# Attention of later blocks two chunks a stop, inside a y, with outputs in the h bank that is free

## The chip, the cores and the metric

The kernel runs on one core of one Trainium2 chip. A core has five engines with a queue each, worked through in order: TensorE (PE: matrix products, with weight loads in a row of their own, PEld), VectorE (DVE), ScalarE (ACT), GpSimd (POOL) and SyncE (SP, which only issues transfers here). Engines wait for each other by semaphores. Matmuls write PSUM; the kernel holds eight tiles of 128 x 512 floats there, called banks here. The metric is the time of one execution in microseconds (us), the median of several runs.

## The reference, cut to what matters

```python
# attention: B, H, S, D = 2, 8, 768, 64, blocks of 64 positions
intra = einsum('bhic,bhjc->bhij', qb, kb) * Dmask      # scores times powers of lam
intra = einsum('bhij,bhjd->bhid', intra, vb)
inter = einsum('bhid,bhde->bhie', qb * lam_pow, kv_state)
out   = intra + inter
kv_state = lam_block * kv_state + einsum('bhsd,bhse->bhde', kb * rev_pow, vb)
# then two feed-forward layers over 1536 tokens, 512 -> 2048 -> 512
h = x @ w_in;  g = elu(h);              x = g @ w_out
h = x @ w_in;  g = P(h) / (Q(h) + 1e-6);  y = g @ w_out  # P cubic, Q of |h| and h*h
```

## The kernel before, in words

The 1536 tokens lie in three blocks of T = 512 (t = 0, 1, 2), and the 2048 hidden features in 16 steps f of 128. A layer is a loop over t and f. A step issues on TensorE h(f) (`mlp_h`, 12 matmuls of 128 x 512, L435: three parts of a product that is split into high and low halves, four slices of the model width each) and then y(f - 2) (`mlp_y`, again 12, L517, into four banks that collect y over all f). Between them ScalarE and VectorE make g from h: L448 and L449 on ScalarE, L450 on VectorE, L452 on ScalarE (high half), L453 on VectorE (low half). Two banks with the tag "h" take turns; four belong to y; the last two, pa0 and pa1, are left for the attention.

Weights of layer 0 come packed and are unpacked on the way in block t = 0: L78, L81 and L84 on VectorE build the weight w_f of a step, L127 on ScalarE makes its high half and L128 on VectorE its low half; h(f + 2) is the first that needs them. In block t = 1 the weights of layer 1 are unpacked by the same three lines and parked in memory (`park_w2`).

The attention of block 0 is done in the start-up, in chunks of 128 positions. That of blocks 1 and 2 is woven into layer 0: chunks 8 to 23 of 64 positions (CS = 64, KB = 12 chunks in a batch) are worked on in t = 0 and 1, one at each of 17 stops (`att_visit`), f = 3, 5, 7, 9, 10, 12, 13, 14, 15 in t = 0 and f = 2, 4, 6, 8, 10, 12, 14, 15 in t = 1. A stop stands between h(f) and y(f - 2). `sm_products(n, d)` issues its matmuls of 64 x 64: for the new chunk n the scores (L340, into half 0 of aa0), and for the chunk d of the stop before the scores times values (L345, half 0 of aa1), the keys' product that goes into the state (L351, half 1 of aa0) and the state times queries (L356, half 0 of aa1). They are issued in pairs that lie in different quarters of the array, 8 steps for a chunk's L340 with L345 and 8 for its L351 with L356. Behind it VectorE masks the scores (L376), POOL scales the queries by the powers in qpow (L371), ScalarE brings out the output (L384, to xr) and VectorE adds up the state (L388); ScalarE scales keys (L365) and state (L395). At the first stop alone, two picks (L333) bring the powers for the other half of the rows into half 1 of aa1, and ScalarE copies them to qpow (L335).

The order within an engine is that of the code in a section under `manual_schedule`; operations of the lists `old`, `new`, `now` and `lows` are placed by hand around the stop. At the start of a block's layer 0, `x_split` makes the halves of x (L57 on ScalarE, L58 on VectorE). SP issues its transfers in the order of the code, and waits with each until its buffer is free.

Of the kernel before, what the change touches and what calls it, by code (L numbers as in the profile page):

```python
# [8 lines left out]
F32 = mybir.dt.float32  # L9
# [20 lines left out]
def fused_kernel(ctx, tc, lam, qkv, w1, w2, ab, out):  # L30
# [16 lines left out]
    ph = ctx.enter_context(tc.tile_pool(name="ph", bufs=2, space=PSUM))  # L47
# [252 lines left out]
    aa_tiles = []  # L300

    def sm_load_qk(k):
# [10 lines left out]
        for b in range(2):  # L313
            chunk[k + b] = {"q": qk[:, :, 0, b * CS:(b + 1) * CS],
                            "k": qk[:, :, 1, (1 - b) * CS:(2 - b) * CS]}

    def sm_load_kv(k):
        c, b, row = k // 2, k % 2, 4 * P
        chunk[k]["kv"] = kv = qq.tile([P, NP, 2, D], F32, tag="kv", name=f"kv{k}")
# [7 lines left out]
    def sm_products(n, d):  # L327

        if not aa_tiles:
# [5 lines left out]
            nc.scalar.activation(out=qpow[:, :, 0:CS], in_=aa_tiles[1][:, 1], func=AF.Copy)  # L335
        pn, pd = chunk.get(n), chunk.get(d)
        for m in range(NP):
            if pn:
                for r in ROWS:
                    nc.tensor.matmul(aa_tiles[0][r, 0, m], lhsT=pn["k"][r, m],  # L340
                                     rhs=pn["q"][r, m], start=True, stop=True,
                                     skip_group_check=True)
            if pd:
                for i, r in enumerate(ROWS):
                    nc.tensor.matmul(aa_tiles[1][ROWS[1 - i], 0, m], lhsT=pd["kv"][r, m, 1],  # L345
                                     rhs=pd["s"][r, m], start=m == 0, stop=d % KB == 0,
                                     skip_group_check=True)
        for m in range(NP):
            if pd and d % KB < KB - 1:
                for r in ROWS:  # L350
                    nc.tensor.matmul(aa_tiles[0][r, 1, m], lhsT=pd["kv"][r, m, 0],  # L351
                                     rhs=pd["kv"][r, m, 1], start=True, stop=True,
                                     skip_group_check=True)
            if pd and d % KB:
                for i, r in enumerate(ROWS):
                    nc.tensor.matmul(aa_tiles[1][ROWS[1 - i], 0, m], lhsT=state[r, m, 0],  # L356
                                     rhs=pd["q"][r, m], start=False, stop=True,
                                     skip_group_check=True)

    def sm_decay_k(n):  # L360

        kv = chunk[n]["kv"]
        if n % KB < KB - 1:
            for m in range(NP):
                nc.scalar.activation(out=kv[:, m, 0], in_=kv[:, m, 0], func=AF.Copy,  # L365
                                     scale=mask64[:, m, CS - 1:CS])

    def sm_decay_q(n):
        q = chunk[n]["q"]
        if n % KB:  # L370
            nc.gpsimd.tensor_tensor(out=q, in0=q, in1=qpow[:, :, 0:CS], op=ALU.mult)  # L371

    def sm_mask(n):
        b = chunk[n]
        b["s"] = s = ap_.tile([P, NP, CS], F32, tag="s", name=f"s{n}")
        nc.vector.tensor_tensor(out=s, in0=aa_tiles[0][:, 0], in1=mask64[:, :, 0:CS], op=ALU.mult)  # L376

    def sm_out(d):

        t, js = d * CS // T, slice(d * CS % T, d * CS % T + CS)  # L380
        if t not in xraw:
            xraw[t] = xr.tile([P, NP, T], F32, tag="xr", name=f"xr{t}")
        first, last = d % KB == 0, d % KB == KB - 1
        nc.scalar.activation(out=xraw[t][:, :, js], in_=aa_tiles[1][:, 0], func=AF.Copy)  # L384
        if first:
            nc.scalar.activation(out=state[:, :, 0], in_=aa_tiles[0][:, 1], func=AF.Copy)
        elif not last:
            nc.vector.tensor_tensor(out=state[:, :, 0], in0=aa_tiles[0][:, 1],  # L388
                                    in1=state[:, :, 1], op=ALU.add)

    def sm_decay_state(d):

        if d % KB not in (0, KB - 1):
            for m in range(NP):
                nc.scalar.activation(out=state[:, m, 1], in_=state[:, m, 0], func=AF.Copy,  # L395
                                     scale=qpow[:, m, CS - 1:CS])

# [102 lines left out]
    def mlp_y(layer, t, f):  # L500
# [27 lines left out]
    with ExitStack() as actx:  # L528
# [4 lines left out]
        qq = actx.enter_context(tc.tile_pool(name="qq", bufs=2))  # L533

# [20 lines left out]
        dmask = ac.tile([P, H, C + 1], F32, name="dmask")  # L555
        qpow = ac.tile([P, NP, C], F32, name="qpow")
        state = ac.tile([P, NP, 2, D], F32, name="state")

        mask64 = dmask.rearrange("p (m h) i -> p m h i", h=2)[:, :, 1, CS:]
# [8 lines left out]
        def make_qpow():  # L568
# [5 lines left out]
            def double(n):  # L574
# [4 lines left out]
        yy, hh = ((py, "y"),) * 2, ((ph, "h"),) * 2  # L579
        pp = (yy, hh, yy, yy, hh, yy, yy, ((ph, "h"), (pa, "pa0")))  # L580
# [4 lines left out]
        loads = [[(sm_load_qk, first), (sm_load_kv, first)], [(sm_load_kv, first + 1)],  # L585
                 [(sm_load_qk, first + 2)]]
        loads += [[(sm_load_kv, k + 1)] + [(sm_load_qk, k + 2)] * (k % 2 == 0 and k + 2 < end)
                  for k in range(first + 1, end - 1)]
        with tc.manual_schedule():
# [17 lines left out]
            for load, k in loads.pop(0):  # L607
                load(k)
# [294 lines left out]
```

## Time and profile before

| | |
|---|---|
| median of 3 runs | 571.9 us (571.89 to 572.04) |
| profiled execution, its own time | 572.56 us |
| span of its profile | 570.8 us |
| TensorE busy | 564.6 us (99%) |
| VectorE busy | 464.7 us (81%) |
| ScalarE busy | 358.5 us (63%) |
| GpSimd busy | 29.8 us (5%) |

A row of a timeline gives the start in us, the duration, the engine, the line and what it writes from what, and in brackets the idle time before it with what ended it. Neighbouring instructions of one kind are merged into one row (x4). A matmul of 64 x 64 in floats of 32 bits stands as two instructions in the trace. In the chain of work that ended last a piece's duration is the time from its start to the start of the next piece, so its rows add up without overlap.

### The profile page before, as it was taken

The numbers are of one execution on the slowest core, as the hardware profiler recorded it, in microseconds if no ns is written. First come the engines' busy times: TensorE is split into PE (matmuls) and PEld (weight loads), VectorE is DVE, ScalarE is ACT, GpSimd is POOL, SyncE is SP. The second block draws the span as 40 slices with busy tenths as digits, with TensorE's granted clock in tenths as the row PEclk, the third lists the DMA queues.
The fourth block names the chain that finished last, engine by engine and source line by source line (L and its number), as shares of the span: only waits on it lengthen the run. The fifth ranks groups of instructions, "written<-read, shape, count | busy, mean of one in ns | idle before, by whom it ended". The sixth has DMA issues, their size and how long they took to land.

```text
span 570.8 us, 9255 instructions
## 1 busy us (share of the span) xinstructions
PE 564.6 (99%) x3550; PEld 464.9 (81%) x3550; DVE 464.7 (81%) x722; ACT 358.5 (63%) x690; POOL 29.8 (5%) x51
## 2 busy tenths in 40 slices
PE   8999999999999999999999999999999999999997
PEld 7877888888888888888888888888888888888885
DVE  6999999965676635877979999888898888898882
ACT  3746646875554545555568976667877666776672
POOL 7401001100100000000000000000000000000000
PEclk9999999999999999999999999999999999999999
DMA  8977677464687513434432500000400000200001
GB/s 291 318 225 243 237 227 214 107 206 128 204 240 229 165 49 136 167 135 177 150 108 78 182 3 1 1 2 0 145 3 2 0 1 0 75 0 1 1 1 74
DMA packets 41215, 64.58 MB, mean 113 GB/s; under 512 B 20178, under 2 KB 20178, under 8 KB 41170
## 3 DMA queue, kind: packets, MB, share of 16 engines
q1 hardware_dynamic: 41168, 63.98, 35.8%
q8 instruction: 28, 0.46, 0.3%
q14 instruction: 17, 0.14, 0.1%
q10 hardware_dynamic: 2, 0.00, 0.0%
HBM read 53.48 MB, written 10.49 MB: 112 GB/s over the span
## 4 chain that ended last, share of the span: by engine, by line
PE 98%; DMA 1%; SPq 0%; ACT 0%; issue 0%
PE h L435 46%; PE y L517 43%; PE y L426 3%; PE aa L340 1%; DMA att<-qkv_in 1%; PE aa L351 1%; PE pa L243 1%; PE pa L209 1%; PE pa L249 0%; PE aa L356 0%; PE aa L345 0%; SPq L192 0%; PE sums L256 0%; PE pa L291 0%; ACT o L487 0%; PE aa L333 0%
## 5 line engine op out<-in xcount | busy, mean ns | idle before, releaser
L435 PE MATMUL h<-xhi,w 128*128 128x512 f32 x768 | 204.8, 389 | 0.0
L517 PE MATMUL y<-ghi,w 128*128 128x512 f32 x712 | 191.8, 392 | 0.0
L435 PEld LDWEIGHTS h<-xhi,w 128*128 128x128 f32 x768 | 143.8, 188 | 30.3 <-DVE w L128 0.4
L517 PEld LDWEIGHTS y<-ghi,w 128*128 128x128 f32 x712 | 132.3, 188 | 27.8
L435 PE MATMUL h<-xlo,w 128*128 128x512 f32 x384 | 102.6, 389 | 0.0
L517 PE MATMUL y<-glo,w 128*128 128x512 f32 x356 | 95.3, 389 | 0.0
L435 PEld LDWEIGHTS h<-xlo,w 128*128 128x128 f32 x384 | 72.1, 188 | 15.0
L517 PEld LDWEIGHTS y<-glo,w 128*128 128x128 f32 x356 | 66.8, 188 | 14.2
L461 ACT ACTIVATE a<-h,babs 128x512 f32<-128x512 f32 x48 | 33.0, 688 | 63.8 <-PE h L435 63.8
L448 ACT ACTIVATE a<-h 128x512 f32<-128x512 f32 x48 | 28.3, 589 | 43.1 <-PE h L435 42.9
L465 DVE SCALAR_TENSOR_TENSOR b<-b,babs,a 128x512 f32<-128x512 f32 x48 | 36.0, 751 | 20.9 <-ACT b L462 20.7
L450 DVE SCALAR_TENSOR_TENSOR b<-a,h 128x512 f32<-128x512 f32 x48 | 32.7, 681 | 15.3 <-ACT a L449 12.1
L452 ACT ACTIVATE ghi<-b 128x512 fp32r<-128x512 f32 x48 | 30.0, 626 | 22.4 <-DVE b L450 22.4
L453 DVE TENSOR_TENSOR glo<-b,ghi 128x512 fp32r<-128x512 f32 x48 | 34.0, 709 | 7.0 <-ACT ghi L452 4.8
L463 ACT ACTIVATE p<-h,cab 128x512 f32<-128x512 f32 x48 | 37.7, 785 | 0.0
L467 ACT ACTIVATE a<-b,one 128x512 f32<-128x512 f32 x48 | 35.0, 729 | 3.1 <-DVE b L465 2.6
L469 DVE SCALAR_TENSOR_TENSOR p<-p,cab,h 128x512 f32<-128x512 f32 x48 | 35.8, 746 | 1.2
L473 DVE SCALAR_TENSOR_TENSOR b<-b,one,a 128x512 f32<-128x512 f32 x48 | 35.8, 746 | 0.1
L475 DVE SCALAR_TENSOR_TENSOR p<-p,cab,a 128x512 f32<-128x512 f32 x48 | 35.8, 746 | 0.0
L58 DVE TENSOR_TENSOR glo<-p,ghi 128x512 fp32r<-128x512 f32 x48 | 33.0, 688 | 3.0 <-PE y L426 1.5
L468 DVE TENSOR_TENSOR p<-p,h 128x512 f32<-128x512 f32 x48 | 32.8, 682 | 2.9 <-ACT p L463 2.9
L477 DVE SCALAR_TENSOR_TENSOR p<-b,p 128x512 f32<-128x512 f32 x48 | 33.1, 690 | 1.2
(88 smaller groups left out, 611.2 us busy)
## 6 DMA issues: line engine op xcount, KB each, us to landing
raw<-w_in SPq DMA_DIRECT2D x64, 512.0 KB, 4.5
att<-qkv_in SPq DMA_DIRECT2D x16, 256.0 KB, 6.0
qk<-qkv_in SPq DMA_DIRECT2D x16, 256.0 KB, 4.3
kv<-qkv_in SPq DMA_DIRECT2D x64, 64.0 KB, 4.0
w2d<-wbuf SPq DMA_DIRECT2D x16, 256.0 KB, 4.5
wbuf<-w2d SPq DMA_DIRECT2D x16, 256.0 KB, 2.8
x2d<-o SPq DMA_DIRECT2D x12, 256.0 KB, 2.3
x2r<-x2d SPq DMA_DIRECT2D x12, 256.0 KB, 3.1
```

What stands on the lines that cost most here:

```text
L58: lo_eng.tensor_tensor(out=lo, in0=src, in1=hi.bitcast(F32), op=ALU.subtract)
L435: nc.tensor.matmul(h, lhsT=w[:, a, 0, k * P:(k + 1) * P], rhs=xs[layer, t, k][b], start=i == k == 0, stop=i == 2 and k == NP - 1)
L453: lambda: nc.vector.tensor_tensor(out=glo, in0=b, in1=ghi.bitcast(F32), op=ALU.subtract)]
L461: nc.scalar.activation(out=a, in_=h, func=AF.Abs, scale=babs[:, 0:1])
L463: nc.scalar.activation(out=p, in_=h, func=AF.Identity, scale=cab[:, 3:4], bias=cab[:, 2:3])
L465: nc.vector.scalar_tensor_tensor(out=b, in0=b, scalar=babs[:, 1:2], in1=a, op0=ALU.mult, op1=ALU.add)
L467: nc.scalar.activation(out=a, in_=b, func=AF.Ln, bias=one[:, 0:1])
L469: nc.vector.scalar_tensor_tensor(out=p, in0=p, scalar=cab[:, 1:2], in1=h, op0=ALU.add, op1=ALU.mult)
L473: nc.vector.scalar_tensor_tensor(out=b, in0=b, scalar=one[:, 0:1], in1=a, op0=ALU.add, op1=ALU.mult)
L475: nc.vector.scalar_tensor_tensor(out=p, in0=p, scalar=cab[:, 0:1], in1=a, op0=ALU.add, op1=ALU.mult)
L477: nc.vector.scalar_tensor_tensor(out=p, in0=b, scalar=2.0, in1=p, op0=ALU.subtract, op1=ALU.mult, reverse0=True)
L517: nc.tensor.matmul(ys[layer, t][m], lhsT=w[:, a, 1, m * P:(m + 1) * P], rhs=g[b], start=f == i == 0, stop=False)
```

## The change

Nine stops take the place of 17, at the steps s = 16 t + f of a list. Each stands inside a y, behind the second of its three parts (8 of 12 matmuls), and works on two chunks. The scores of both chunks n, n + 1 fill aa0 (L344). The keys' products (L359) are made for the chunks n - 1 and n, one chunk behind the loads rather than with the outputs, and lie in the two halves of aa1. The outputs of the two chunks of the stop before (L349, L364) go into a third place, `ax`: the h bank that the next h will take. One L395 of 128 x 512 brings them out, one mask L386 of 128 x 512 takes the place of two, and one L378 on POOL scales two chunks of queries. The state has a third copy, is summed in L405 (first time in L403) and scaled in L412; keys are scaled in L373. The large tables move into a weight slot; what the stops need of them lies in two small tiles (mask64, pow64), which two POOL copies and the one L335 fill. The banks for h have tags of their own, h0 and h1. In the new kernel L435 is L451, L517 is L533, and L448, L449, L450, L452, L453 are L464, L465, L466, L468, L469. TensorE's instructions of the stops, in the program's own count, go from 17 groups to nine.

```diff
-    ph = ctx.enter_context(tc.tile_pool(name="ph", bufs=2, space=PSUM))
+    ph = ctx.enter_context(tc.tile_pool(name="ph", bufs=1, space=PSUM))
...
-            nc.scalar.activation(out=qpow[:, :, 0:CS], in_=aa_tiles[1][:, 1], func=AF.Copy)
...
+            nc.scalar.activation(out=pow64, in_=aa_tiles[1][:, 1], func=AF.Copy)
+        if d is not None:
+            aa_x[0] = spare.rearrange("p (m x i) -> p m x i", x=2, m=NP)
+        for j in range(2):
+            pn = chunk.get(n + j) if n is not None else None
+            pd = chunk.get(d + j) if d is not None else None
+            for m in range(NP):
+                if pn:
+                    for r in ROWS:
+                        nc.tensor.matmul(aa_tiles[0][r, j, m], lhsT=pn["k"][r, m],
+                                         rhs=pn["q"][r, m], start=True, stop=True,
+                                         skip_group_check=True)
+                if pd:
+                    for i, r in enumerate(ROWS):
+                        nc.tensor.matmul(aa_x[0][ROWS[1 - i], m, j], lhsT=pd["kv"][r, m, 1],
+                                         rhs=pd["s"][r, m], start=j == m == 0,
+                                         stop=(d + j) % KB == 0, skip_group_check=True)
+        for j in range(2):
+            c = n + j - 1 if n is not None else None
+            kv = chunk[c]["kv"] if c in chunk and c % KB < KB - 1 else None
+            pd = chunk.get(d + j) if d is not None and (d + j) % KB else None
+            for m in range(NP):
+                if kv is not None:
+                    for r in ROWS:
+                        nc.tensor.matmul(aa_tiles[1][r, j, m], lhsT=kv[r, m, 0],
+                                         rhs=kv[r, m, 1], start=True, stop=True,
+                                         skip_group_check=True)
+                if pd:
+                    for i, r in enumerate(ROWS):
+                        nc.tensor.matmul(aa_x[0][ROWS[1 - i], m, j], lhsT=state[r, m, j],
+                                         rhs=pd["q"][r, m], start=False, stop=True,
+                                         skip_group_check=True)
...
+        nc.scalar.activation(out=xraw[t][:, :, js].rearrange("p m (b i) -> p m b i", b=2),
+                             in_=aa_x[0], func=AF.Copy)
...
+        tables = slot(1, [P, H * (C + 1) + NP * C], F32, "tables")
...
+        at = [3, 6, 9, 12, 14, NF + 2, NF + 6, NF + 10, NF + 14]
...
-        h_pool = lambda: (ph, "h")
+        h_pool = lambda: (ph, f"h{nh.pop()}")
+        nh = [f % 2 for f in range(2 * NF)][::-1]
...
+        def att_visit(s, f):
+
+            v = at.index(s)
+            spare = ph.tile([P, T], F32, tag=f"h{(f + 1) % 2}", name=f"ax{s}") if v else None
+            n = pairs[v] if v < len(pairs) else None
+            d = pairs[v - 1] if v else None
+            sm_products(n, d, spare)
+            if d is not None:
+                sm_out(d)
             if n is not None:
                 sm_mask(n)
                 sm_decay_q(n)
...
             if d is not None:
+                if n is not None:
+                    sm_state(n)
...
                 if len(queue) > LAG:
-                    mlp_y(*queue.pop(0))
+                    mlp_y(*queue.pop(0), between=(lambda: att_visit(s, f)) if s in at else None)
+                for load, k in loads.get(s, ()):
+                    load(k)
...
-    def mlp_y(layer, t, f):
+    def mlp_y(layer, t, f, between=None):
...
+            if between and i == 1:
+                between()
...
-        return ((ph, "h"), (ph, "h"), (pa, "pa0"), (pa, "pa1"))[nh[0] % 4]
+        return ((ph, "h0"), (ph, "h1"), (pa, "pa0"), (pa, "pa1"))[nh[0] % 4]
```

How the rows stand, at three places. In a name such as h_0_3 the numbers are block and step, and a number behind it the program's count of buffers.

TensorE at the first stop (f = 3), before: the end of h(3), the picks, the scores, and the start of y(1).

```order
L435 MATMUL h_0_3_586<-xhi_0_0_261,w_1_508 128x512 x2
L435 MATMUL h_0_3_586<-xhi_0_1_285,w_1_508 128x512 x2
L333 MATMUL aa_613<-dmask,tabs 64x256 x2
L340 MATMUL aa_612<-qk_200 64x64 x8
L517 MATMUL y_0_0_570<-ghi_0_1_504,w_1_508 128x512
L517 MATMUL y_0_1_571<-ghi_0_1_504,w_1_508 128x512
```

After, from the second part of y(1), with the semaphores that a row waits for in brackets (DMAHW: a transfer's):

```order
L533 MATMUL y_0_0_576<-glo_0_1_510,w_1_513 128x512 [waits DVE_50]
L533 MATMUL y_0_1_577<-glo_0_1_510,w_1_513 128x512
L533 MATMUL y_0_2_578<-glo_0_1_510,w_1_513 128x512
L533 MATMUL y_0_3_579<-glo_0_1_510,w_1_513 128x512
L333 MATMUL aa_640<-mask_162,tabs 64x256 [waits Pool_50] x2
L344 MATMUL aa_639<-qk_204 64x64 [waits DMAHW0_50,PE_50]
L344 MATMUL aa_639<-qk_204 64x64 [waits DMAHW1_50]
L344 MATMUL aa_639<-qk_204 64x64 x14
L359 MATMUL aa_640<-kv_207 64x64 [waits DMAHW2_50,Activation_50]
L359 MATMUL aa_640<-kv_207 64x64 [waits DMAHW4_50]
L359 MATMUL aa_640<-kv_207 64x64 x2
L359 MATMUL aa_640<-kv_207 64x64 [waits DMAHW3_50]
```

The scores and picks now stand inside y(1), and behind them L359, with a wait for ScalarE, stands ahead of y(1)'s last part.

ScalarE at the same stop, before: L448 and L449 belong to h(3), L335 is the copy of the picked powers.

```order
L448 ACTIVATE a_0_3_601<-h_0_3_586 128x512
L449 ACTIVATE a_0_3_601<-a_0_3_601 128x512
L335 ACTIVATE qpow<-aa_613 128x4x64
L365 ACTIVATE kv_203<-kv_203,dmask 128x64 x4
L127 ACTIVATE w_3_605<-w_3_606 128x1024
L452 ACTIVATE ghi_0_3_599<-b_0_3_602 128x512
```

After:

```order
L464 ACTIVATE a_0_3_610<-h_0_3_595 128x512
L465 ACTIVATE a_0_3_610<-a_0_3_610 128x512
L127 ACTIVATE w_3_614<-w_3_615 128x1024
L335 ACTIVATE pow_163<-aa_640 128x256
L468 ACTIVATE ghi_0_3_608<-b_0_3_611 128x512
```

The copy L335 moved from ahead of L127 of w_3 to behind it.

VectorE at the change from block 1 to block 2, before: L450 belongs to h(14) and h(15) of block 1, L58 makes the low half of x, L78, L81 and L84 unpack weights of layer 1.

```order
L450 SCALAR_TENSOR_TENSOR b_1_14_2479<-a_1_14_2478,h_1_14_2463 128x512
L453 TENSOR_TENSOR glo_1_14_2477<-b_1_14_2479,ghi_1_14_2476 128x512
L58 TENSOR_TENSOR xlo_2_0_2598<-xr_1715,xhi_2_0_2597 128x512 x2
L58 TENSOR_TENSOR xlo_2_1_2604<-xr_1715,xhi_2_1_2603 128x512 x2
L450 SCALAR_TENSOR_TENSOR b_1_15_2550<-a_1_15_2549,h_1_15_2534 128x512
L78 TENSOR_SCALAR wbuf<-raw_0_0_2627 128x512
L81 SCALAR_TENSOR_TENSOR wbuf<-raw_0_0_2627,wbuf 128x512
L453 TENSOR_TENSOR glo_1_15_2548<-b_1_15_2550,ghi_1_15_2547 128x512
L84 SCALAR_TENSOR_TENSOR wbuf<-raw_0_0_2627,wbuf 128x512
```

After (L466 is what L450 was, L469 what L453 was):

```order
L469 TENSOR_TENSOR glo_1_14_2479<-b_1_14_2481,ghi_1_14_2478 128x512
L78 TENSOR_SCALAR wbuf<-raw_0_0_2610 128x512
L81 SCALAR_TENSOR_TENSOR wbuf<-raw_0_0_2610,wbuf 128x512
L84 SCALAR_TENSOR_TENSOR wbuf<-raw_0_0_2610,wbuf 128x512
L78 TENSOR_SCALAR wbuf<-raw_0_1_2612 128x512
L58 TENSOR_TENSOR xlo_2_0_2580<-xr_1785,xhi_2_0_2579 128x512 x2
L58 TENSOR_TENSOR xlo_2_1_2586<-xr_1785,xhi_2_1_2585 128x512 x2
L466 SCALAR_TENSOR_TENSOR b_1_15_2549<-a_1_15_2548,h_1_15_2533 128x512
L81 SCALAR_TENSOR_TENSOR wbuf<-raw_0_1_2612,wbuf 128x512
```

Four steps on the weights moved ahead of L58 and of L466 of h(15).

## Rows read from the trace of the kernel before

**Rows 1.** The page: TensorE's busy time, and the shares of the chain by engine.
```profile
PE 564.6 (99%) x3550; PEld 464.9 (81%) x3550; DVE 464.7 (81%) x722; ACT 358.5 (63%) x690; POOL 29.8 (5%) x51
...
PE 98%; DMA 1%; SPq 0%; ACT 0%; issue 0%
```

**Rows 2.** Windows (columns: busy us of each engine): blocks 0 and 1.
```profile
36.00:72.00 36.00, 36.00 (x289) 29.25 (x286) 34.53 (x42) 22.73 (x51) 3.15 (x3) 1.00 0.74 237
...
118.00:224.00 106.00, 106.00 (x903) 86.60 (x902) 65.01 (x111) 54.12 (x128) 6.22 (x7) 1.00 0.55 162
```

**Rows 3.** The chain in order of time (start us, us, what): block 0, some pieces.
```profile
35.58 0.58 PE aa L333 x4
...
45.01 2.95 PE h L435 x12
...
52.03 2.72 PE h L435 x12
...
60.19 0.20 PE aa L340 x2
...
60.41 0.04 PE aa L340 x2
...
61.28 2.95 PE y L517 x12
```

**Rows 4.** Timeline of ScalarE (start us, us, instruction [idle before]): h(3), first stop.
```profile
38.90 0.63 ACT L449 ACTIVATE a<-a 128x512 f32<-128x512 f32 x1
39.44 0.37 ACT L335 ACTIVATE qpow<-aa 128x256 f32<-128x256 f32 x1
...
43.05 1.06 ACT L127 ACTIVATE w<-w 128x1024 fp32r<-128x1024 f32 x1 [2.29 <-DVE w L84]
```

**Rows 5.** Timeline of VectorE: the same stretch.
```profile
39.12 0.69 DVE L453 TENSOR_TENSOR glo<-b,ghi 128x512 fp32r<-128x512 f32 x1
39.72 0.42 DVE L376 TENSOR_TENSOR s<-aa,dmask 128x256 f32<-128x256 f32 x1
40.05 1.70 DVE L81 SCALAR_TENSOR_TENSOR w<-raw,w 128x1024 int32<-128x1024 int32 x1
41.79 1.22 DVE L84 SCALAR_TENSOR_TENSOR w<-raw,w 128x1024 int32<-128x1024 int32 x1
...
44.88 0.70 DVE L78 TENSOR_SCALAR w<-raw 128x1024 int32<-128x1024 int32 x1 [1.26 <-DMA raw<-w_in]
45.49 1.22 DVE L128 TENSOR_TENSOR w<-w,w 128x1024 fp32r<-128x1024 f32 x1
```

**Rows 6.** Timelines: VectorE's L84 of f = 6; ScalarE's eviction of a bank.
```profile
59.85 1.23 DVE L84 SCALAR_TENSOR_TENSOR w<-raw,w 128x1024 int32<-128x1024 int32 x1
...
224.56 0.61 ACT L487 ACTIVATE o<-y 128x512 f32<-128x512 f32 x1
```

**Rows 7.** Timelines at the end of block 1: VectorE, SP's loads.
```profile
211.48 2.50 DVE L58 TENSOR_TENSOR xlo<-xr,xhi 128x512 fp32r<-128x512 f32 x4 [5.16 <-ACT xhi L57]
...
215.16 0.43 DVE L78 TENSOR_SCALAR wbuf<-raw 128x512 int32<-128x512 int32 x1 [0.58 <-PE y L517]
215.62 0.69 DVE L81 SCALAR_TENSOR_TENSOR wbuf<-raw,wbuf 128x512 int32<-128x512 int32 x1
...
210.45 1.69 SPq L114 DMA_DIRECT2D raw<-w_in  x2
```

**Rows 8.** Windows of the program's end (PEclk: granted clock); timeline of TensorE's start.
```profile
566.00:567.00 1.00, 0.85 (x4) 0.38 (x2) 0.00 (x0) 0.24 (x2) 0.00 (x0) 1.00 0.35 131
...
569.00:570.00 1.00, 0.00 (x0) 0.00 (x0) 0.00 (x0) 0.00 (x0) 0.00 (x0) 1.00 0.07 23
570.00:570.50 0.50, 0.00 (x0) 0.00 (x0) 0.00 (x0) 0.00 (x0) 0.00 (x0) 0.59 0.00 0
...
5.92 1.13 PE L243 MATMUL pa<-att 128*64 128x128 f32 x8
...
9.17 0.66 PE L243 MATMUL pa<-att 128*64 128x128 f32 x8
```

More of the change, by code (lines that the diff above doesn't have):

```diff
@@ L348, in sm_products @@
[L348 to L358, printed above, removed]
+            nc.scalar.activation(out=pow64, in_=aa_tiles[1][:, 1], func=AF.Copy)
@@ L391, in sm_decay_state, with sm_state @@
-    def sm_decay_state(d):
-        if d % KB not in (0, KB - 1):
+        nc.scalar.activation(out=xraw[t][:, :, js].rearrange("p m (b i) -> p m b i", b=2),
+                             in_=aa_x[0], func=AF.Copy)
+    def sm_state(n):
+        if n - 1 in chunk and n % KB:
+            j = n % 2
+            if n % KB == 1:
+                nc.scalar.activation(out=state[:, :, j], in_=aa_tiles[1][:, j], func=AF.Copy)
+            else:
+                nc.vector.tensor_tensor(out=state[:, :, j], in0=aa_tiles[1][:, j],
+                                        in1=state[:, :, 2], op=ALU.add)
@@ L584, in fused_kernel @@
         first, end = todo[0], todo[-1] + 1
[L585 to L588, printed above, removed]
+        at = [3, 6, 9, 12, 14, NF + 2, NF + 6, NF + 10, NF + 14]
+        pairs = list(range(first, end, 2))
+        loads = {}
+        for i, k in enumerate(pairs[1:]):
+            s0 = at[i] if i else 1
+            for j, load in enumerate(((sm_load_kv, k - 1), (sm_load_qk, k), (sm_load_kv, k))):
+                loads.setdefault(s0 + (j if i == 0 else j // 2), []).append(load)
+        loads.setdefault(at[-2], []).append((sm_load_kv, end - 1))
+        work, late, states = {}, {}, {}
+        for v, s in enumerate(at[:-1]):
+            k = first + 2 * v
+            if v:
+                late.setdefault(s - 1, []).append((sm_decay_k, k - 1))
+                work.setdefault(s, []).append((sm_decay_k, k))
+            work.setdefault(s + 1, []).append((sm_decay_state, k))
+            states[s + 1] = k + 1
+            work.setdefault(s + 2 + (s + 2 == NF), []).append((sm_decay_state, k + 1))
         with tc.manual_schedule():
@@ L606, in fused_kernel @@
             load_pair(1)
-            for load, k in loads.pop(0):
-                load(k)
+            for load in (sm_load_qk, sm_load_kv):
+                load(first)
             def s_part(i):
@@ L711, in fused_kernel @@
         queue = []
-        def att_visit(due, more):
-            n = todo.pop(0) if more and todo else None
-            d = due.pop() if due else None
-            sm_products(n, d)
+        def att_visit(s, f):
[6 more added lines that the diff above has]
+                sm_out(d)
             if n is not None:
@@ L792, in fused_kernel @@
                                 FULL + 1: (FULL + 3, NF - 3)}[f])
-                if loads and (f in visits[t][1 - t:] or t == 0 and f in (1, 2)):
-                    for load, k in loads.pop(0):
-                        load(k)
                 if t == 0 and f == 3:
```

103 lines of the change are left out of this document (43 added, 60 removed).

## The prediction

> **What bounds the kernel now.** I read the page's busy times and its chain that ended last first, then windows of single stages, then the chain piece by piece, and last the timelines of the engines that would have to wait. The first two views leave one engine: TensorE is busy for 564.6 of 570.8 us and makes 98% of the chain [rows 1]. So a stop costs what it adds to TensorE's row of matmuls, and a wait costs only if TensorE itself stands still. The windows show who could make it wait [rows 2]: from 36 to 72 us, in block 0, VectorE is busy for 34.53 of 36 us, but from 118 to 224 us for only 65.01 of 106. In block 0 it runs behind: its last step on the weights of f = 6 (L84, 59.85 + 1.23) ends at 61.08 [rows 6], while h of f = 6 started at 52.03 [rows 3]. That is a lag of 9 us, almost two steps, and the piece of h at 45.01 took 2.95 instead of 2.72 us [rows 3] since its last third met L128 of w_3, which ran from 45.49 to 46.7 [rows 5]. So TensorE is the bound, and VectorE just fails to be one in block 0.
>
> **The change part by part.**
>
> Fewer stops. In the chain [rows 3] a stop begins at 60.19, its second step at 60.41, and y goes on at 61.28: fifteen steps in 0.87 us, 0.058 each, and a first step of 0.22, so 0.16 us to enter. The y behind it takes 2.95 us where twelve such matmuls take 2.72: 0.23 to leave. A stop costs 0.39 beside its steps. 17 become 9: -8 x 0.39 = **-3.1 us**. I take entry and exit inside a y as the same, since the same two shapes meet there.
>
> The steps. Before, the first stop has 8 steps, fifteen have 16, the last 16: 264. After, the first has 24 (16 of scores, 8 of the first chunk's keys' product), seven have 32 and the last 32: 280. 16 x 0.058 = **+0.9 us**.
>
> The new wait at the first stop. The order shows on TensorE: 8 of the 12 matmuls of y(1), the two picks, 16 scores, then L359, which waits for ScalarE. L359 (j = 1) writes the half of aa1 from which L335 copies the picked powers. Before, nothing on TensorE followed that copy so closely, and ScalarE ran it at 39.44, right behind L449 of h(3) (38.90) [rows 4]. Now it stands behind L127 of w_3, which ran at 43.05 after VectorE's L84 [rows 4]. When does TensorE arrive? h(3) ends at 35.58 [rows 3]; 8 matmuls are two thirds of 2.72, 1.81; picks 0.58; sixteen steps 0.92: **38.9**. When is the copy done? VectorE starts L453 at 39.12; the mask L376 that followed at 39.72 now stands behind L84, so L81 starts at 39.72 [rows 5]. It took 1.70 there; L84 of the same size took 1.22. With 1.22 for both, L84 ends at 42.2; L127 adds 1.06, L335 0.37 [rows 4]: **43.6**. The stall is 43.6 - 38.9 = **+4.7 us**. With 1.70 for L81 and some start-up of each engine it is 5.6; were VectorE's whole queue a step of 1.2 us earlier it would be 3.5. Queued behind L359 on TensorE are the last third of y(1), h(4) and everything else: nothing hides it. VectorE doesn't gain all of it, since its L78 of w_4 waits until 44.88 for its weights from memory [rows 5]. What it keeps is that h(5) no longer meets L128: **-0.2**.
>
> Later stops in block 0. Outputs now lie in the bank of the next h, so h(f+1) waits for L395, which stands on ScalarE behind L127 of w_f, and that behind L84. An eviction of that size took 0.61 us [rows 6]. At f = 6 h starts, by the terms above, at 52.03 + 4.7 + 0.9 - 0.4 - 0.9 (the old stop at f = 5 took 16 steps and its 0.39) - 0.2, about 56.1; its 12 and 8 matmuls end at 60.6, the stop at 62.6 (0.16 and 32 steps), and h(7) is due at 63.8. L84 ends near 61.1 as before, L127 near 62.2, L395 at 63.3: half a microsecond to spare, because the first stall has halved the lag. f = 9 comes out alike, f = 12 and 14, where stops follow each other closely and one more decay lies on ScalarE, a little short. I take **+0.4** for all four, with 0 and 1.5 as ends (1.5 is one L127 and one eviction too late).
>
> Block 1. VectorE has 41 of 106 us free [rows 2], L127 isn't there: nothing, and 0.5 if one eviction meets its h.
>
> Into block 2. h of (2, 0) now takes the same bank as h of (1, 15), so it waits for L466 of (1, 15). In the new order VectorE has L78, L81, L84 and L78 of the next layer's weights ahead of the four L58 and that L466. The weights are asked for behind the last use of the stop's buffers (210.45), and L78 ran at 215.16 [rows 7], so 4.7 us later; then 0.43 for each L78, 0.69 for L81 and as much for L84 (the same form), 2.50 for the four L58 [rows 7] and 0.7 for L466 make 5.4, which gives 10.1 us from the last full stop's end V to the end of L466. TensorE has a third of a y with its exit (1.14) and three groups of 2.72: V + 9.3. So **+0.8**, ends 0 and 2.
>
> At nothing: masks (8 of twice the size for 16), the decay of two chunks on POOL (needed a stop later), the state's second copy, and the two table copies in the start-up; the work between two stops hides them. On SP the loads of keys and queries move behind the y, so weights of the same step pass them; a load that waits for a buffer holds the next step's weights, which are wanted two steps on. If that cover is gone it costs up to a microsecond in block 0; it widens the top.
>
> Sum: -3.1 + 0.9 - 0.2 + 4.7 + 0.4 + 0.8 = **+3.5 us**. The profiled execution took 572.56 us, 0.66 over the median of 571.9, and its span is 570.8; so the profiled one would come to 576.1, the median to **575.4**.
>
> The clock. At the end of the program TensorE's last matmul ended near 566.85; the granted clock read 1.00 up to 570 and 0.59 on average in the half microsecond behind it [rows 8], so it fell from 2.4 towards 1.2 GHz after TensorE had stood idle for some 3 us. In the stall it stands idle for 4.7 us, so the clock may have fallen when y(1) goes on. Work at the lower level takes longer: eight L243 took 1.13 us at 5.92, early in the program, and 0.66 at 9.17 [rows 8]. I bound the slow stretch by none and 6 us, so a loss of 0 to 3 at half the speed, and take the middle, 1.5; since VectorE gains that time, the 0.4 at the later stops goes. That makes +4.6 in place of +3.5. The Trainium skill ("TensorE: Matmul & The Clock Gate", section "Part 1: The HAM clock gate") says that the clock drops to 1.2 GHz when the array has been idle and returns after busy work; the end of this trace agrees for the drop, and no stall inside the kernel is there to show the return. By that rule the time would be that of case B below, without it the forecast.
>
> **The rivals.** (B) Same stalls, and the clock falls: 576.5. For it the end of the trace; against it that this is a single instance, in which TensorE was idle for good.
> (D) VectorE's lag isn't cured by the first stall, since it waits for its weights (44.88) and for the delayed h(4). Without any cure, h(7) would be due near 59.1 while L395 can't end before 62.7: 3.6 us there, and as much again at f = 9. With half of it at both, some 4 us on the forecast: 579.5.
> (C) The other side, faster: VectorE's lag is shorter from the start, because the start-up's work is laid out anew and L84 of w_3 ends before 37.5 (38.9 less L127 and L335) instead of 43.0. Then L335 is done when TensorE arrives, L395 is early as well, and what is left is -3.1 + 0.9 + 0.8 = -1.4: 570.5. It decides from a lag under 4.7 us at f = 3. Against it: VectorE has no 5 us free ahead of that point in rows 5, nor between 36 and 72 us.
> (E) The copy comes some 2.5 us earlier than I place it (the wait ends with a shorter queue on VectorE): 573, no measurable change.
>
> **How the numbers follow.** Stall without clock 0.42, B 0.32, D 0.11, C 0.09, E 0.06. The likeliest is 575.4. Its own ends: 571.9 - 2.4 + 3.5 = 573.0, and 571.9 - 2.4 + 5.6 + 1.5 + 2 = 578.6. The range 573.2 to 579.2 holds it and B, and leaves out C, most of E and half of D, together about 0.2. A measurement of this kernel tells 0.2%, 1.1 us, from no change. Slower by more than that: 0.42 + 0.32 + 0.11 = 0.85; within it 0.06; faster 0.09.
>
> **What would show it.** In the new profile: nine groups of steps, each 32 steps in about 2.0 us; in the waits, TensorE at L359 waiting once for ScalarE's L335, between 3.5 and 5.6 us, ending near 43.6; L127 of w_3 right ahead of L335; no wait of h at f = 7 and 10 above half a microsecond; one of h for L466 near 220 us under 2 us; and the granted clock of the stretch from 43 to 50 us, 1.00 or less. A wait at L359 under 2 us, or waits of 3 us at f = 7, would prove the sum wrong.

## The result and the profile of the changed kernel

The changed kernel takes 576.77 us in the median of 6 runs (576.5 to 578.39), the kernel before, run beside it, 571.97 us (571.81 to 573.43). The ratio is 1.0083, with a 95% interval from 1.0068 to 1.0098: slower by 4.8 us, or 0.8%. The forecast was 575.4 with the range 573.2 to 579.2; case B, the same stalls with the clock falling, stood at 576.5. The profiled execution took 578.39 us and spans 576.6.

The page, its busy times and its chain, the answer to [rows 1]:

```profile
PE 566.5 (98%) x3550; PEld 469.1 (81%) x3550; DVE 462.6 (80%) x714; ACT 359.5 (62%) x682; POOL 26.7 (5%) x45
...
PE 94%; DVE 3%; DMA 1%; ACT 1%; SPq 0%; issue 0%
```

TensorE's busy time grew by 1.9 us and its span by 5.8, so 3.9 us more are idle; 3% of the chain now lie on VectorE. What TensorE waited for (us in total, times, longest):

```profile
PE aa L359 <- ACT pow L335: 4.7, 1, 4.7
PE pa L628 <- DVE wbuf L558: 1.1, 1, 1.1
PE pa L209 <- DMA att<-qkv_in: 0.7, 1, 0.7
```

The two lower rows belong to the start-up, which waited about as long before. The upper one is the wait of the first stop. ScalarE's timeline there, the answer to [rows 4], and at the next stop:

```profile
40.48 0.63 ACT L465 ACTIVATE a<-a 128x512 f32<-128x512 f32 x1
43.73 1.06 ACT L127 ACTIVATE w<-w 128x1024 fp32r<-128x1024 f32 x1 [2.62 <-DVE w L84]
44.70 0.36 ACT L335 ACTIVATE pow<-aa 128x256 f32<-128x256 f32 x1
...
66.51 0.60 ACT L395 ACTIVATE xr<-ax 128x512 f32<-128x512 f32 x1 [0.81 <-PE ax L364]
```

VectorE's, the answer to [rows 5]:

```profile
40.62 0.68 DVE L469 TENSOR_TENSOR glo<-b,ghi 128x512 fp32r<-128x512 f32 x1
41.23 1.22 DVE L81 SCALAR_TENSOR_TENSOR w<-raw,w 128x1024 int32<-128x1024 int32 x1
42.48 1.22 DVE L84 SCALAR_TENSOR_TENSOR w<-raw,w 128x1024 int32<-128x1024 int32 x1
43.62 0.68 DVE L386 TENSOR_TENSOR s<-aa,mask 128x512 f32<-128x512 f32 x1
...
45.77 1.25 DVE L78 TENSOR_SCALAR w<-raw 128x1024 int32<-128x1024 int32 x1 [0.87 <-DMA raw<-w_in]
```

The copy L335 starts where L127 of w_3 ends, and that starts where L84 ends. The mask L386, which has taken over from L376, now comes behind L84, and L81 takes 1.22 us. Everything lies 1.5 us later than in the prediction, since in this execution the start-up was longer by that much; L243, for one, still took 1.12 us at 9.44, where it took 0.66 at 9.17 before [rows 8]:

```profile
9.44 1.12 PE L243 MATMUL pa<-att 128*64 128x128 f32 x8
```

The chain in order of time, from the end of the wait to the next stop, and that stop's first and last pieces, the answer to [rows 3]:

```profile
45.12 1.12 PE aa L359 x16
46.23 2.00 PE y L533 x4
48.23 3.47 PE h L451 x12
51.70 2.72 PE y L533 x12
...
64.40 0.20 PE aa L344 x2
...
64.61 0.04 PE aa L344 x2
...
66.42 1.12 PE y L533 x4
67.55 2.73 PE h L451 x12
```

Behind the wait the 16 rows of the keys' product take 1.12 us, the last third of y 2.00, and h(4) 3.47; the later pieces of the same kinds take 1.12 for the third of y with its exit and 2.73 for an h. Why, the windows show (columns as in [rows 2]: busy us of TensorE, weight loads, VectorE, ScalarE and GpSimd, then the granted clock):

```profile
41.00:42.00 1.00, 0.00 (x0) 0.00 (x0) 1.00 (x2) 0.11 (x1) 0.00 (x0) 1.00 0.95 147
42.00:43.00 1.00, 0.00 (x0) 0.00 (x0) 0.97 (x2) 0.00 (x0) 0.00 (x0) 0.89 1.03 313
43.00:44.00 1.00, 0.00 (x0) 0.00 (x0) 1.00 (x2) 0.27 (x1) 0.00 (x0) 0.50 0.81 119
...
48.00:49.00 1.00, 1.00 (x4) 0.77 (x3) 1.00 (x3) 0.00 (x0) 0.00 (x0) 0.50 0.99 393
49.00:50.00 1.00, 1.00 (x5) 0.81 (x4) 1.00 (x2) 0.00 (x0) 0.00 (x0) 0.70 1.03 414
```

TensorE is idle from 40.4; the granted clock drops to 0.50, the level of 1.2 GHz, near 42.8, stays there while TensorE works again, and is back near 49.6. The rule of the Trainium skill that the prediction weighed ("TensorE: Matmul & The Clock Gate", section "Part 1: The HAM clock gate") is borne out here in both directions, with the return that no row of before showed.

How long the clock is low differs from one execution to the next of the same kernel. The mean granted clock of the whole execution, kept for every one, shows it: the changed kernel read 0.997 in the fastest of its six and 0.993 or 0.994 in the other five; the kernel before reads 0.998 to 1.000 in every execution on record.

Into block 2, VectorE and SP, the answer to [rows 7]:

```profile
216.30 0.43 DVE L78 TENSOR_SCALAR wbuf<-raw 128x512 int32<-128x512 int32 x1 [1.69 <-DMA raw<-w_in]
...
218.43 2.50 DVE L58 TENSOR_TENSOR xlo<-xr,xhi 128x512 fp32r<-128x512 f32 x4
220.85 0.68 DVE L466 SCALAR_TENSOR_TENSOR b<-a,h 128x512 f32<-128x512 f32 x1
```
```profile
212.87 0.81 SPq L114 DMA_DIRECT2D raw<-w_in  x2
```

SP asks for the weights at 212.87, L78 gets the first at 216.30, L466 of h(15) ends at 221.53, and h of block 2 starts in its turn near 222.0, without a wait.

One view settles the account better than any row. I cut every profiled execution at three matmuls: the first of the first h, the first of y(15) of block 0, that of block 1. The stretches, in us, one execution of each kernel, with what the sum of the merged stops alone would give (-0.6 for block 0's stops and steps, -0.2 for h(5), -1.6 for block 1's stops):

| kernel | start-up | block 0 | block 1 | rest |
|---|---|---|---|---|
| before | 21.04 | 102.62 | 97.59 | 349.55 |
| before, copy late (e6) | 20.37 | 102.35 | 97.59 | 349.49 |
| stops merged, by the sum | | 101.8 | 96.0 | 349.55 |
| changed | 22.57 | 108.68 | 96.09 | 349.26 |
| dummies in the stall (e3) | 20.58 | 106.76 | 96.69 | 349.27 |
| copy early (e1) | 20.77 | 107.61 | 96.18 | 349.24 |
| copy in the same step (e2) | 21.58 | 108.96 | 96.10 | 349.26 |
| less on VectorE (e7) | 20.48 | 103.74 | 96.19 | 349.29 |
| outputs first (e4) | 20.78 | 104.62 | 96.13 | 349.27 |
| decays early (e5) | 21.22 | 103.54 | 96.40 | 349.24 |
| x first (e8) | 20.37 | 102.94 | 97.55 | 349.24 |
| x, then w (e9) | 20.55 | 103.31 | 96.26 | 349.28 |
| the same, less on VectorE (e10) | 20.83 | 101.91 | 96.13 | 349.33 |

Block 1 gives what was promised for it, block 0 loses 6.1 us. The two kernels with the old stops differ by 0.27 us in block 0, which says how far a single execution can be trusted there. The start-up varies from run to run by more than some of the effects; that is why the medians of the experiments don't always follow the sums of the other three columns.

### The profile page after: what moved, and what is told of

The parts are those of the page before. It is cut to its first block, busy times and chain, and to the rows that moved or that the text cites. A ratio compares the mean times of both kernels' runs of the same rounds, so it can differ in the third digit from the quotient of the medians.

```text
span 576.6 us, 9227 instructions
## 1 busy us (share of the span) xinstructions
PE 566.5 (98%) x3550; PEld 469.1 (81%) x3550; DVE 462.6 (80%) x714; ACT 359.5 (62%) x682; POOL 26.7 (5%) x45
## 4 chain that ended last, share of the span: by engine, by line
PE 94%; DVE 3%; DMA 1%; ACT 1%; SPq 0%; issue 0%
PE h L451 44%; PE y L533 42%; PE y L442 3%; PE aa L344 1%; DMA att<-qkv_in 1%; PE aa L359 1%; PE pa L209 1%; PE pa L243 1%; DVE w L81 1%; DVE w L128 1%; DVE w L84 1%; PE ax L364 1%; PE pa L249 0%; PE ax L349 0%; DVE w L78 0%; DVE glo L469 0%
## 5 line engine op out<-in xcount | busy, mean ns | idle before, releaser
L451 PE MATMUL h<-xhi,w 128*128 128x512 f32 x768 | 205.6, 391 | 0.0
L533 PE MATMUL y<-ghi,w 128*128 128x512 f32 x712 | 191.7, 392 | 0.0
L451 PEld LDWEIGHTS h<-xhi,w 128*128 128x128 f32 x768 | 144.5, 188 | 30.5
L533 PEld LDWEIGHTS y<-ghi,w 128*128 128x128 f32 x712 | 133.4, 188 | 27.9
L451 PE MATMUL h<-xlo,w 128*128 128x512 f32 x384 | 102.7, 389 | 0.0
L533 PE MATMUL y<-glo,w 128*128 128x512 f32 x356 | 95.1, 389 | 0.0
L451 PEld LDWEIGHTS h<-xlo,w 128*128 128x128 f32 x384 | 72.2, 188 | 15.1
L533 PEld LDWEIGHTS y<-glo,w 128*128 128x128 f32 x356 | 66.8, 188 | 13.9
L464 ACT ACTIVATE a<-h 128x512 f32<-128x512 f32 x48 | 28.5, 593 | 53.0 <-PE h L451 52.6
L466 DVE SCALAR_TENSOR_TENSOR b<-a,h 128x512 f32<-128x512 f32 x48 | 32.7, 681 | 24.8 <-ACT a L465 19.8
L468 ACT ACTIVATE ghi<-b 128x512 fp32r<-128x512 f32 x48 | 30.0, 627 | 22.2 <-DVE b L466 22.2
L469 DVE TENSOR_TENSOR glo<-b,ghi 128x512 fp32r<-128x512 f32 x48 | 32.8, 685 | 9.3 <-ACT ghi L468 7.1
L58 DVE TENSOR_TENSOR glo<-p,ghi 128x512 fp32r<-128x512 f32 x48 | 33.0, 687 | 3.0 <-PE y L442 1.5
```

What stands on the lines that cost most here:

```text
L58: lo_eng.tensor_tensor(out=lo, in0=src, in1=hi.bitcast(F32), op=ALU.subtract)
L451: nc.tensor.matmul(h, lhsT=w[:, a, 0, k * P:(k + 1) * P], rhs=xs[layer, t, k][b], start=i == k == 0, stop=i == 2 and k == NP - 1)
L469: lambda: nc.vector.tensor_tensor(out=glo, in0=b, in1=ghi.bitcast(F32), op=ALU.subtract)]
```

## The experiments

In the experiments the lines are shifted by a few: L361 or L364 is the changed kernel's L359, L397 its L395, L334 or L337 its L335, L375 its L373, L453 or L456 its L451, L538 its L533, and L471 in e3 its L466.

### Is the low clock a cost of its own?

```diff
+        if d is None:
+            pad = ph.tile([P, T], F32, tag="h0", name="pad")
+            for _ in range(20):
+                nc.tensor.matmul(pad, lhsT=wt[0, 0][:, 0, 0, 0:P], rhs=xs[0, 0, 0][0],
+                                 start=True, stop=True)
```

> The changed kernel with 20 matmuls of 128 x 512 more, between the scores and the keys' product of the first stop, into the bank of h that is free there; their result is not read. They take 20 x 0.227 = 4.5 us, about the length of the wait. Theory (the wait itself costs 4.7 us, and the idle time costs another 2.3 us through the clock: keys' products 1.12 instead of 0.46, the rest of y 2.00 instead of 1.14, h 3.47 instead of 2.72): the wait shrinks to about 0.2 us, the work behind it runs at clock 1.00, time 2.3 us under the changed kernel, near 574.5. Rival (the slow work behind the wait has another cause, such as transfers or VectorE): the same pieces stay long, time within 0.5 us of 576.8.

Measured: 575.19 us (575.10 to 575.39), ratio 1.0055 [1.0040, 1.0070]. Its chain at the place:

```profile
38.51 4.76 PE pad L355 x20
43.26 0.63 PE aa L364 x16
43.89 1.12 PE y L538 x4
45.02 2.73 PE h L456 x12
```

The dummies fill the wait, and behind them the third of y takes 1.12 instead of 2.00 and h 2.73 instead of 3.47. Block 0 falls from 108.68 to 106.76, 1.9 us. The mean clock is 0.999 or 1.000 in all four executions. So the wait and the clock are two costs: 4.7 us of waiting and about 2 us of slow work behind it. Matmuls that compute nothing make the kernel faster here.

The time is 0.7 us above the 574.5 expected. Part of it is a wait at the change to block 2 that the changed kernel's profiled execution doesn't have:

```profile
PE h L456 <- DVE b L471: 0.4, 1, 0.4
```

It is the wait for L466 that the prediction put at 0.8.

### Does the wait go away if the copy is early?

```diff
+                if s == 2:          # e2: s == 3
+                    sm_picks()      # the two picks and L335, taken out of sm_products
```

> The changed kernel with one edit: the two picks and the copy of the powers (L335) are issued one step earlier, behind h of f = 2, so that the copy lies on ScalarE ahead of L127 of w_2. Nothing is left out. Theory (the lag of VectorE is the cause and the copy only its first victim): the wait of 4.7 us at the keys' product is gone, but the lag of 9 us is then not cured, and h of f = 7 waits some 3.5 us for the eviction of the outputs, which stands behind L127 of w_6 (h due near 59.3 on the time line of before, eviction done near 62.8). Time 573.2 if the clock holds, up to 575 if it falls again in that wait. Rival (only the copy's place was wrong): no wait of TensorE above 0.5 us is left, time 569.5 to 569.8, clock 1.00 throughout.

Measured: 576.48 us (575.63 to 578.40), ratio 1.0081 [1.0060, 1.0103], as slow as the changed kernel and above the 575 that was expected at most. TensorE's waits have this new row; ScalarE shows what it waited for, and the chain and a window what followed:

```profile
PE h L453 <- ACT xr L397: 3.6, 1, 3.6
```
```profile
61.16 1.06 ACT L127 ACTIVATE w<-w 128x1024 fp32r<-128x1024 f32 x1 [2.77 <-DVE w L84]
62.12 0.58 ACT L397 ACTIVATE xr<-ax 128x512 f32<-128x512 f32 x1
```
```profile
62.75 4.62 PE h L453 x12
```
```profile
62.00:63.00 1.00, 0.25 (x1) 0.25 (x2) 1.00 (x3) 1.00 (x3) 0.00 (x0) 1.00 0.84 217
63.00:64.00 1.00, 1.00 (x4) 0.76 (x4) 1.00 (x2) 1.00 (x5) 0.00 (x0) 0.56 1.01 385
64.00:65.00 1.00, 1.00 (x4) 0.81 (x3) 1.00 (x3) 0.28 (x2) 0.00 (x0) 0.50 1.01 397
```

The first stop no longer waits. The lag of VectorE is still there, and h(7) pays for it: the eviction L397 stands behind L127 of w_6 (61.16), and h(7) waits 3.6 us for it, as long as predicted in rival D. The clock falls here too, and h(7) takes 4.62 us, 1.9 more than its 2.72. The profiled execution is the fastest of the four: two took 575.63 and 575.77 at a mean clock of 0.997, the other two 577.18 and 578.40 at 0.993, so there the clock was low for longer than the rows show. That, with the 1.9 us on top of the wait, is how the time left the expected range.

> The changed kernel with picks and copy issued right behind h of f = 3, so that the copy is ahead of L127 of w_3 on ScalarE, as it was before. Nothing is left out. Theory: ScalarE is free for the copy at 39.4 and done at 39.8 on the time line of before, so the keys' product waits about 0.9 us; the rest of the 3.5 us, some 2.6, is waited at h of f = 7. Two short waits in place of a long one: the clock stays at 1.00, time near 573.2. Rival (the clock falls by the sum of the idle time): low clock in a window behind h of f = 7, time 575 or more. Rival (only the copy's place): 570.4 to 570.8.

Measured: 577.57 us (573.82 to 579.59), ratio 1.0079 [1.0046, 1.0112].

```profile
PE h L453 <- ACT xr L397: 4.0, 1, 4.0
...
PE aa L361 <- ACT pow L334: 0.6, 1, 0.6
```

The first wait is 0.6 us, near the 0.9 expected; the second is 4.0, and not the rest of a fixed sum of 3.5. Here the expectation failed: the 0.6 us waited first took nothing off the second wait, and behind that the clock fell in the profiled execution (h(7) took 4.61 us). The rival had the clock fall by the sum of the idle time; its time and the low clock behind h(7) came, but e1 shows that 3.6 us in one piece are enough without a sum. In one execution of the six the mean clock read 1.000, and that one took 573.82 us, near the 573.2 expected with the clock at 1.00; in the others it read 0.993 to 0.997, and they took 575.05 to 579.59. Taking the copy's place for the cause, as the wait's row suggests, would have led to a version that is no faster.

### Does a late copy cost in itself?

```diff
-            nc.scalar.activation(out=qpow[:, :, 0:CS], in_=aa_tiles[1][:, 1], func=AF.Copy)
+            pend.append(...)        # the copy and L371, run behind L127 of w_3
```

> The kernel before with one edit: the copy of the powers (L335) and the scaling of the queries of that chunk stand behind L127 of w_3, as the copy does in the changed kernel. Nothing is left out. Theory (a late copy costs only because the keys' product of the same stop overwrites what it reads): TensorE doesn't wait, the copy runs near 43.6, time within 0.3 us of before. Rival (a late copy holds up ScalarE or POOL in itself): slower by a microsecond or more.

Measured: 572.05 us, ratio 0.9995 [0.9986, 1.0004], no change, and no wait of TensorE at any stop.

```profile
41.89 1.06 ACT L127 ACTIVATE w<-w 128x1024 fp32r<-128x1024 f32 x1 [2.07 <-DVE w L84]
42.85 0.37 ACT L335 ACTIVATE qpow<-aa 128x256 f32<-128x256 f32 x1
```

The copy runs behind L127, and nobody on TensorE needs aa1 before the stop at f = 5. It takes the keys' product in the same stop to make the place on ScalarE matter.

### Is it VectorE's lag?

```diff
+        if f:
+            ops[1] = lambda: None   # L81, the second unpacking step of a pair of weights
```

> The changed kernel with one of the three unpacking steps (L81) left out for the weights of f = 1 to 9, 11, 12 and 13 of layer 0, so that these weights are wrong; the order of everything else is as in the changed kernel. It takes 1.22 us a step off VectorE. Theory (VectorE's lag is what makes the order on ScalarE cost): L84 of w_3 ends some 3.7 us earlier, the wait at the keys' product shrinks from 4.7 to about 1 us, the clock stays at 1.00, no wait at the later stops, time 571.9 - 2.2 + 1.0 = 570.7. Rival (the order alone costs, whatever the lag): a wait of 3 us or more, the clock falls, 575 or more.

The kernel leaves out L81, so its weights are wrong; only its time counts. Measured: 571.95 us (571.17 to 573.33), ratio 1.0000 [0.9991, 1.0008]. The one wait at a stop, and ScalarE there:

```profile
PE aa L361 <- ACT pow L337: 1.7, 1, 1.7
```
```profile
38.64 1.06 ACT L127 ACTIVATE w<-w 128x1024 fp32r<-128x1024 f32 x1 [1.37 <-DVE w L84]
39.60 0.36 ACT L337 ACTIVATE pow<-aa 128x256 f32<-128x256 f32 x1
```

The order is that of the changed kernel, and with 1.22 us a step off VectorE the wait falls from 4.7 to 1.7 us, the clock of this execution stays at 1.00 there, h waits at no later stop, and 4.8 us are gone. The expected 570.7 was missed, for one thing because 1.7 us were waited, not 1.0 (L127 came at 38.64; it was expected at 38.5 on the time line of before, and this run's start-up is 0.6 us shorter). For another, three of the ten executions have a mean clock of 0.996 or 0.997 and took 572.83 to 573.33 us, the seven others 0.999 or 1.000 and 571.17 to 572.17; where the clock was low in those three, no trace shows. It is the lag that gives the place in the queue its price.

### Where does the saving of block 0 go?

Four versions take away one wait after the other by order alone, each on top of the last. First, besides the early copy, L127 of a stop's step goes behind the eviction:

```diff
-                    run(w, len(w) - 1)
+                    run(w, len(w) - 1 - hold)   # hold: a stop of block 0 from f = 6 on
...
+                if hold:                        # behind mlp_y
+                    for w in now:
+                        run(w, len(w) - 1)
```

> The changed kernel with the copy early (as behind h of f = 2) and, at the stops of block 0 from f = 6 on, L127 of that step's weights issued behind the eviction of the outputs instead of ahead of it. Nothing is left out. Theory (the place on ScalarE behind late weights is what costs, at the first stop and then at h): no wait of TensorE above 0.5 us at any stop, clock 1.00, time 571.9 - 3.1 + 0.9 = 569.7. Rival (VectorE is the bound of block 0 by now, whatever ScalarE does): h waits for L128 of the weights two steps back again and again, 0.2 to 0.5 us each, time 570.5 to 572.

Measured: 572.48 us (571.39 to 573.26), ratio 1.0004 [0.9994, 1.0013]: the long waits are gone, but with them 4.3 us and not the 7 that lead to the 569.7 expected. What is left in TensorE's waits, and ScalarE ahead of it:

```profile
PE aa L361 <- ACT kv L375: 0.6, 1, 0.6
```
```profile
106.45 1.06 ACT L127 ACTIVATE w<-wbuf 128x1024 fp32r<-128x1024 f32 x1 [1.50 <-DVE wbuf L84]
...
108.89 1.05 ACT L375 ACTIVATE kv<-kv,mask 128x64 f32<-128x64 f32 x4
...
110.99 0.58 ACT L397 ACTIVATE xr<-ax 128x512 f32<-128x512 f32 x1
```

At f = 14 the keys' product waits for L375, which stands behind L127 of w_13, and the eviction L397 behind both. Neither theory holds as put: it isn't L128, but again ScalarE's queue behind late weights. The next version moves the scaling and the picks, and loads chunk 16's keys a step earlier:

```diff
-                loads.setdefault(s0 + (j if i == 0 else j // 2), []).append(load)
+                loads.setdefault(s0 + (j if i == 0 else j // 2 * (i != 3)), []).append(load)
...
+        late[13] = work.pop(14)[:1] + late[13] + [(sm_decay_k, 16)]
...
+                    sm_picks()          # behind att_hand, at f = 1
```

> As the kernel with the copy early and the outputs' eviction ahead of L127, with three more moves: the picks stand right behind the last small products of block 0 (f = 1), so that they don't pay an entry and an exit of their own (0.39 us); the scaling of the state and of the keys of chunk 16, which the stop at f = 14 waited for (0.6 to 0.8 us, with slower steps behind it), is issued one step earlier, ahead of L127 of w_13; keys of chunk 16 are loaded a step earlier for that. Theory (what is left at the stops of block 0 is ScalarE's order): the stop at f = 14 takes 2.0 us instead of 3.3, no wait of h behind it, time 572.5 - 0.4 - 1.5 = 570.6. Rival (VectorE's work bounds block 0, so that a wait taken away comes back at the next step that needs its weights): 572.0 to 572.5.

Measured: 571.85 us (571.30 to 574.03), ratio 1.0000 [0.9988, 1.0011], between the 570.6 expected and the rival's 572.0. The stop at f = 14 is down to 2.0 us, and the next victim shows, h(1, 0), whose first four matmuls took 2.07 us in TensorE's timeline:

```profile
117.02 0.63 ACT L127 ACTIVATE w<-wbuf 128x512 fp32r<-128x512 f32 x1 [0.67 <-DVE wbuf L84]
117.56 2.18 ACT L57 ACTIVATE xhi<-xr 128x512 fp32r<-128x512 f32 x4
```

L57, which makes x of block 1, stands behind L127 of w_15.

```diff
-                    run(w, len(w) - 1 - hold)
+                    run(w, len(w) - 1 - (hold or s == NF - 1))
```

> As the kernel with the early decays, with one more move: L127 of w_15 is issued behind the four L57 that make x of block 1, instead of ahead of them. In the run before, h(1, 0) was stretched by about 1.1 us since L57 stood behind that L127 (117.02), and it behind VectorE's L84 (116.29). Theory (the saving of 2.2 us is there and each piece of it is given back where ScalarE's next wanted step stands behind late weights): h(1, 0) runs in 2.9 us or less, L57 starts near 116.4, time 1.1 us under the run before, 570.8, and 0.2% under the kernel before. Rival (VectorE's L58 or L128 of w_15 takes over as what h or y waits for): within 0.4 us of the run before, 571.5 to 572.3.

Measured: 572.70 us (571.45 to 573.59), ratio 1.0008 [0.9999, 1.0018]. Block 0 fell by 0.6 to 102.94, half of the 1.1 expected, and block 1 rose by 1.15 to 97.55: with L127 far behind, L128, the parking steps and the low half of g(15) were late, and y(15) waited 0.4 us for it. The rival was right in kind; the time lies above its 572.3 as well.

```diff
                         x_split(0, t, m)
+                    run(lows, 1)        # L127 of w_15, right behind the four L57
```

> As the kernel with x of block 1 first, but L127 of w_15 directly behind the four L57, so that L128, the parking steps and the low half of g(15) behind it on VectorE aren't late. Nothing is left out. By stretches between the first h, the first matmul of y(15) of block 0, that of block 1, and the end: before 102.6, 97.6 and 349.6 us; theory: 102.9, 96.2 and 349.3, so 1.2 us less than before in what lies behind the start-up, time 570.8 if the start-up is the same. Rival (block 0 stays bound by VectorE and the loss moves on once more): block 1 stays at 97 or more, time 571.5 or more.

Measured: 571.20 us (570.26 to 572.28), ratio 0.9983 [0.9973, 0.9993], 0.4 over the expected 570.8. This version beats both kernels, the one before by 0.17%, the changed one by about 1%. Block 0 stays at 103.31, 0.4 over the expectation and 1.5 over the sum. At f = 9 ScalarE works without a gap from an L127 behind L84 (74.03) to the eviction L397, which ends at 78.20, and h starts at 78.25; the rest of the 1.5 was not taken apart.

The last version leaves out L81 as e7 does, on top of all these moves.

> The kernel with x, then w (all moves on ScalarE made), and in it the unpacking step L81 left out for the weights of f = 1 to 9, 11, 12 and 13 of layer 0, so that these weights are wrong; everything else in the same order. Theory (the saving of the merged stops in block 0 is real, and VectorE's lag alone takes it back): no wait of TensorE at any stop, the stretch of block 0 at 102.6 - 0.6 (four stops fewer, 16 steps more) - 0.2 (wait for L128 gone) = 101.8 us, that of block 1 at 96.1, time 569.7 to 569.9. Rival (the entry or exit inside a y costs more than between h and y, or the count of steps is wrong): block 0 at 102.4 or more with no wait to be seen.

Measured: 569.98 us (569.95 to 570.24), ratio 0.9963 [0.9950, 0.9977]. Block 0 takes 101.91 us and block 1 96.13, within 0.1 of the expectation, with no wait of TensorE at any stop. The time is 0.1 above the 569.9 expected at most. VectorE in the window from 36 to 72 us, against 34.53 of 36 in [rows 2]:

```profile
36.00:72.00 36.00, 36.00 (x318) 29.75 (x318) 27.81 (x36) 22.22 (x46) 2.58 (x2) 1.00 0.91 280
```

So the sum for the merged stops is met to 0.1 us in both blocks, in one execution, and 0.27 is what block 0 differed by between the two kernels with the old stops. In block 0 the saving exists, and VectorE's lag takes it back. The kernel before was not run without L81; of its own block 0 that could take little, since the one loss there to VectorE in its chain is the 0.2 at h(5).

## Why the prediction was right, point by point

**The bound.** Right: TensorE is the bound, and VectorE's lag in block 0 is what stops it. e7 against the changed kernel, and e10 against e9, show it by taking work off VectorE alone.

**Merged stops and steps, -3.1 and +0.9, and -0.2 for h(5).** Right: -1.5 in block 1 (four stops fewer at the same count of steps: -1.6), -0.7 in block 0 with VectorE relieved (-0.6 and -0.2). Entry and exit inside a y cost what they cost between h and y. The rest of the program became 0.3 us shorter, which the sum did not have; no run looked for its cause.

**The wait at the first stop, +4.7.** Right, in size and place: 4.7 us at L359 for L335, with L127 right ahead and L81 at 1.22. That ScalarE doesn't start the copy although its input is there since the picks is what the Trainium skill says of the queues ("PSUM — Partial Sum Buffer", section "Engine vs sequencer instructions": strictly first in, first out), and the rows at 40.48, 43.73 and 44.70 agree.

**Later stops, +0.4.** Too high by 0.4: the changed kernel waits at none. At f = 6 the eviction ended at 67.11 and h started at 67.55, 0.44 us to spare, against the 0.5 worked out; f = 12 and 14 were fine as well. The reason given, that the first stall cures the lag, is what e1 shows from the other side: without it h(7) waits 3.6 us, the price worked out for rival D. In e3, where VectorE gains no time from slow work on TensorE, no later stop of block 0 waits either.

**Into block 2, +0.8.** Wrong in size, at one link: L78 came 3.6 us behind the stop's end (216.30 - 212.72), not 4.7. The figure was read from [rows 7], a single pair of loads, which took 4.6 and 5.5 us from issue to landing; in the changed kernel they took 3.2 and 4.4. L466 then ended half a microsecond early. In e3 the loads took 3.3 and 5.5 us, and the wait was there, at 0.4. So the wait is real, and its size hangs on the loads.

**The clock.** This is the step on which the forecast of 575.4 failed. The likeliest case had no loss by it, and what came was B: granted 0.50 from 42.8 to 49.6 us. Its loss was 0.66 + 0.86 + 0.75 = 2.3 us (the keys' product, the third of y, h(4)), above the 1.5 taken from the middle of bounds and inside their end at 3. e3 shows it as a cost apart. Weighing "a single instance" against a longer idle time of the same kind was too careful, though e1, e2 and e7 show that the clock does not do the same in every execution. The row that the prediction took for work at the lower level, L243 at 5.92, stands where the clock's column reads 1.00, so it did not show that price; the rows behind the stall do. And e3, the same stall with the clock at 1.00, is the likeliest case as it was put, and takes 575.19 us.

**The sum.** Block 0: 4.7 + 2.3 - 0.6 - 0.2 = 6.2, measured 6.1. With -1.5 and -0.3 that is +4.3 without the start-up; the medians differ by 4.8. The half microsecond left may lie in the start-up, which varied between 20.4 and 22.6 us among the profiled executions, or in the clock; that the changed start-up is on average slower was not shown, and it stays open. The forecast of +3.5 was 0.4 + 0.8 too high at the two small waits and 2.3 too low at the clock. That B's 576.5 comes within 0.3 us of the measured 576.77 is in part luck: it holds 0.8 for block 2 that did not come, and a clock loss that is 0.8 too small.

**Rivals.** D's wait at h(7) happens once the first stall is taken away (e1, e2); its second, at f = 9, does not. C's point of decision, a lag under 4.7 us, was nearly reached by cutting VectorE's work in e7, with 1.7 us of waiting left. With ScalarE's moves as well, e10 takes 569.98, beside C's 570.5. E did not happen.

## What to carry to other kernels

Before an eviction or a copy is put behind other work in an engine's queue, ask what that work waits for: on an engine that runs in order, a buffer's release inherits the lag of whatever stands ahead. A wait that appears is often the first victim of a lag and not its cause; take it away, and look where the lag lands next, before counting the gain. And a long idle time of TensorE can be paid twice, as here, once as a wait and once in slower matmuls behind it, so the account of a stall needs the granted clock beside it, of several executions and not of the profiled one alone.

## What was not expected of the hardware

The drop came late in e1: TensorE stood idle from 59.1 to 62.75, the window from 62 to 63 us still reads 1.00, and the drop comes behind it, on work that had begun again. In the profiled executions the three single waits of 3.6, 4.0 and 4.7 us each cost 1.9 to 2.3 us more that way, and the one of 1.7 us in e7 nothing. But it isn't the same each time: by the mean clocks, the clock cost e2 nothing in one execution of six, cost e1 more in two of four than in the profiled one, and three of e7's ten had a low clock somewhere. And in the start-up the same matmuls took 0.66 or 1.12 us from one execution to the next at the same place, while the clock's column read 1.00, so there the rows' durations tell more than that column.
